# Whole-head and half-head cache loads in elements two to four of a two-layer decode kernel

## The chip, the cores and the metric

The kernel runs on one core of a Trainium2 chip. The metric is the device time of one execution in microseconds; the median over the runs is compared. The profile is of one execution. Its engines are PE (matmuls; PEld are its weight loads), DVE (VectorE), ACT (ScalarE), POOL (GpSimd) and SP (SyncE, which issues nearly all transfers).

## The reference

A decode step for four batch elements goes through two equal layers, each an attention block over a cache and a feed-forward block. The weights and the cache are the same in both layers.

```python
B, Sq, D = 4, 1, 512
Hq, Hkv, Sk, Dh = 32, 8, 4096, 128          # cache: [B, Hkv, Sk, Dh], bf16

def _A_ref(x, k_cache, v_cache, wq, wo):
    q = (x @ wq).reshape(B, Sq, Hq, Dh)      # moved to [B, Hq, Sq, Dh]
    k = jnp.repeat(k_cache, rep, axis=1)     # four query heads share a key head
    v = jnp.repeat(v_cache, rep, axis=1)
    scores = jnp.einsum("bhqd,bhkd->bhqk", q, k) * (Dh ** -0.5)
    p = _softmax(scores, axis=-1)
    o = jnp.einsum("bhqk,bhkd->bhqd", p, v)
    return o.reshape(B, Sq, Hq * Dh) @ wo

def _B_ref(x, w_gate, w_up, w_down):
    return (_gelu(x @ w_gate) * (x @ w_up)) @ w_down

x = x + _A_ref(_layernorm(x), k_cache, v_cache, wq, wo)
x = x + _B_ref(_layernorm(x), w_gate, w_up, w_down)
x = x + _A_ref(_layernorm(x), k_cache, v_cache, wq, wo)
x = x + _B_ref(_layernorm(x), w_gate, w_up, w_down)
```

The result does not depend on the order of the 4096 cache positions, so a kernel may put them on the partitions in any way that keys and values share.

## The kernel before

**Tiles.** One head of keys or values is 4096 x 128 in bf16, 1 MB. It is held as two tiles (t = 0 and 1, "half heads") of 512 KB, each 128 partitions x 16 positions x 128. In the usual layout tile t holds one contiguous half of the head, and each partition reads one run of 4 KB. In element one (b = 0), the heads of the first group (`whole`) are laid out over the partitions as whole heads: a partition reads 32 positions, one run of 8 KB, and both tiles come with one transfer (`load_head`).

**Groups and elements.** The eight key heads form two groups of four. The elements are worked through in order, and layer two of element b is woven into layer one of element b + 1 (`attend`), so that the keys of element b can stay on the chip for both. Layer one takes the groups in the order `first_groups[b]` (0, 1 for elements one and three; 1, 0 for two and four), layer two in the opposite order (`second_groups`). In each part of the code the first group of the order at hand is gx, the second gy.

**Keys.** There are 16 key tiles on the chip (8 MB): `KW` for group 0 and `KP` for group 1. `place` says which tile holds which half head. In `attend` layer two's scoring of the previous element goes over gx, then gy, with t = 0 and then t = 1 (line 592); each pass frees four tiles, and four half heads of the next element are loaded into them (line 518). DVE then turns each key tile in place in the order of loading (`turn`, line 537, 1.2 us a tile), and layer one scores them. Scoring a tile takes four matmuls of 32 columns. The columns of the PE array follow the head, so that tiles of different heads go side by side. Layer one scores gx one tile at a time and gy in runs of three tiles and one (`last_alone`).

Between elements one and two there are no free tiles to load into. `Early` therefore parks three key tiles of group 0 in PSUM and elsewhere, loads three half heads into their places, and brings the parked ones back, on ACT, DVE and POOL (lines 565 to 570), as scoring frees others.

**Values.** Eight value tiles form a ring (`VRing`, in pairs `VP`). `ring.seq` is the list of half heads in the order in which they are to be loaded; `pump` issues the next load when a slot is free, and every value step (`Values.step`, `Streamed.fill`) frees one and pumps. Layer two keeps the last three half heads of layer one (`kept`), parks two more in PSUM (`apart`), and reads the other eleven again: three of the second group (`own`) and the eight of the first group (`other`). The eight are consumed during the next dense block, one at each `prev.fill()`, between the steps of the feed-forward block (lines 309 and 791). In the last element, three transfers of 1 MB go into the space of the query weights instead (`pump_head`, line 724), and one head goes into two freed key tiles.

**Queue.** All loads are issued by SP in program order. A load waits on SP for the matmul that last read its tile, and for an earlier transfer that used the same semaphore.

**The end.** `attend_last` takes the values of the last element in the order kept, own, apart, other. After heads 4 and 5 of the last group come the output rows of four heads (`rows.heads`, line 405), then head 6 with its rows, then head 7, whose output goes through line 275. The last feed-forward block follows (`dense_last`).

Of the kernel before, what the change touches and what calls it, by code (L numbers as in the profile page):

```python
# [15 lines left out]
P = 128  # L16
# [14 lines left out]
WD_PARTS = (0, 6, 10, 12, 13, 14)  # L31
ROWS_A = 8
# [4 lines left out]
def kernel(  # L37
# [58 lines left out]
    KW = [wts.tile([P, NT, CH, Dh], BF16, name=f"kw{s}") for s in range(GH)]  # L96
    KP = [[wts.tile([P, 2, CH, Dh], BF16, name=f"kp{t}_{j}") for j in range(GH // 2)]
          for t in range(NT)]
# [22 lines left out]
    place = {(s, t): (KW[s], t) for s in range(GH) for t in range(NT)}  # L121
    place.update({(GH + s, t): (KP[t][s // 2], s % 2) for s in range(GH) for t in range(NT)})

    def k_tile(i, t):
        pair, n = place[i, t]
        return pair[:, n]
# [15 lines left out]
    def whole(b, kvh):  # L142
        return b == 0 and kvh < GH

    def load_head(cache, kvh, to):
        dq.dma_start(out=to.rearrange("p t c d -> p (t c d)"),
                     in_=cache[0, kvh].rearrange("(p r) d -> p (r d)", p=P))

    def cache_tile(cache, b, kvh, t):
        if whole(b, kvh):  # L150
            return cache[b, kvh].rearrange("(p t c) d -> t p c d", t=NT, p=P)[t]
        return cache[b, kvh].rearrange("(t p c) d -> t p c d", t=NT, p=P)[t]
# [287 lines left out]
    def flat(t, nb):  # L440
        return t[:, :, 0] if nb == 1 else t
# [52 lines left out]
    class Keys:  # L494


        def __init__(self, b, groups):
            self.b, self.groups, self.nl, self.nt = b, groups, 0, 0

        def tile(self, n):  # L500
            g, u = divmod(n, TG)
            if whole(self.b, self.groups[g] * GH):
                s, t = divmod(u, NT)
            else:
                t, s = divmod(u, GH)
            return self.groups[g] * GH + s, t

        def load_heads(self, count):
            for _ in range(count):
                kvh, t = self.tile(self.nl)  # L510
                self.nl += NT
                load_head(A_k_cache, kvh, KW[kvh])

        def load(self, count):
            for _ in range(count):
                kvh, t = self.tile(self.nl)
                self.nl += 1
                dq.dma_start(out=k_tile(kvh, t), in_=cache_tile(A_k_cache, self.b, kvh, t))

        def load_pairs(self, count):  # L520
            for _ in range(count):
                kvh, t = self.tile(self.nl)
                (to, n), (other, m) = place[kvh, t], place[kvh + 1, t]
                if to is not other or (n, m) != (0, 1):
                    self.load(2)
                    continue
                self.nl += 2
                pair = A_k_cache[self.b, kvh:kvh + 2].rearrange("h (t p c) d -> t p h c d",
                                                                t=NT, p=P)
                dq.dma_start(out=to[:], in_=pair[t])  # L530

        def turn(self, count=1):
            for _ in range(count):
                kvh, t = self.tile(self.nt)
                self.nt += 1
                words = k_tile(kvh, t).rearrange("p c d -> p (c d)").bitcast(FP32)
                nc.vector.transpose(out=words, in_=words)  # L537
# [40 lines left out]
    together = (tuple(range(GH)),)  # L578
    singly = tuple((s,) for s in range(GH))
    last_alone = (tuple(range(GH - 1)), (GH - 1,))  # L580

    def scores(sc, g, t, runs=together):
        for run in runs:
            scores_of(sc, g, [(s, t) for s in run])

    def scores_of(sc, g, run):
        for be in range(BE):
            for s, t in run:
                n = s * BE + be
                w0 = n * 2 * W + (W if t == 0 else 0)  # L590
                kt = k_tile(g * GH + s, t).rearrange("p c (b j e) -> p c b j e", b=NB, e=2)
# [90 lines left out]
    class VRing:  # L682
# [9 lines left out]
        def pump(self, spare=None):  # L692
            free = self.free if spare is None else spare
            while self.at < len(self.seq) and free:
                key = self.seq[self.at]
                if key[0] == 1 and whole(*key[1:3]):
                    own = [free.pop(0) for _ in range(NT)]
                    n = [i for i, v in enumerate(slots) if v is own[0]][0]
                    assert n % NT == 0 and own[1] is slots[n + 1]
                    load_head(A_v_cache, key[2], VP[n // NT])  # L700
                    for t in range(NT):
                        assert self.seq[self.at] == key[:3] + (t,)
                        self.at += 1
                        self.ready[key[:3] + (t,)] = (own[t], spare is None)
                    continue
                self.at += 1
                v = free.pop(0)
                dq.dma_start(out=v, in_=cache_tile(A_v_cache, *key[1:]))
                self.ready[key] = (v, spare is None)
# [11 lines left out]
        def pump_head(self, keys, pair):  # L721
            (layer, b, kvh, t), other = keys
            assert t == 0 and other == (layer, b, kvh, 1)
            dq.dma_start(out=pair,
                         in_=A_v_cache[b, kvh].rearrange("(t p c) d -> p t c d", t=NT, p=P))
# [233 lines left out]
    def attend_first():  # L959
# [11 lines left out]
        keys.load_heads(GH)  # L971
        load_wq(gy)
        keys.load(TG)
# [36 lines left out]
        scores(sc1, gy, 0, last_alone)  # L1010
        keys.turn(4)
        vals.step(3)
        scores(sc1, gy, 1, last_alone)
# [25 lines left out]
    class Early:  # L1039


        def __init__(self, b, groups):
# [3 lines left out]
            self.own = dict(place)  # L1046
            flat = [k_tile(c + s, last).rearrange("p c d -> p (c d)") for s in range(GH)]
            self.two = [Parked(flat[2], [(ps_h, "h", 2), (ps_x, "x", 2)]),
                        Parked(flat[3], [(pool, "ot", 2) for pool in ps_ot])]
            self.one = Parked(flat[1], [(ps_sc, "sc", 2), (pep, "pe", 4), (pep, "pl", 4, 1)])  # L1050
            place[a, 0], place[a + 1, 0] = self.own[c + 2, last], self.own[c + 3, last]
            place[a + 2, 0] = self.own[c + 1, last]
            self.keys = Keys(b, groups)
            self.keys.load_pairs(1)
            self.keys.load(1)
# [33 lines left out]
        def scores(self, sc, qy, norm):  # L1089
            gx, gy, own, keys = self.gx, self.gy, self.own, self.keys  # L1090
            a, c, last = gx * GH, gy * GH, NT - 1

            def home(i, t, freed):
                place[i, t] = own[freed]
                return k_tile(i, t).rearrange("p c d -> p (c d)")

            def load(i, t, freed):
                home(i, t, freed)
                assert keys.tile(keys.nl) == (i, t)
                keys.load(1)  # L1100

            def first(run):
                now = {(a + s, t): place[a + s, t] for s, t in run}
                place.update({k: own[k] for k in now})
                scores_of(sc, gx, run)
                place.update(now)
# [9 lines left out]
            to = home(c + 1, last, (a + 1, 0))  # L1116
            self.one.back(to, 1, nc.vector)
            self.one.back(to, 2, nc.gpsimd)
            self.two[0].back(home(c + 2, last, (a, 0)), 2)
# [453 lines left out]
```

## Time and profile before

| | |
|---|---|
| median of 3 runs | 268.06 us (267.89 to 269.08) |
| profiled execution | 268.99 us, of which span 267.2 us |
| mean granted TensorE clock | 0.866 |
| PE / DVE / ACT / POOL busy | 195.1 / 182.2 / 66.0 / 3.9 us |
| PE weight loads | 114.8 us |
| bytes read from HBM | 102.50 MB, 384 GB/s over the span |
| key loads of 512 KB / 1024 KB | 56 / 4 |
| value loads of 512 KB into the ring / 1024 KB into the ring / 1024 KB into weight space | 89 / 4 / 3 |

The rows of the page give each engine's busy share, the 40 slices show how it lies over the span, and the list of transfers gives sizes and the time from issue to landing. That time includes the time spent behind earlier transfers of the queue. The groups by line show how often an instruction ran, its mean duration, and what ended the idle time before it. Matmuls overlap, so that the sum of their durations is more than the time they take.

### The profile page before, as it was taken

Reading aid. Unit: us, or ns where it says so; the run is one execution under the profiler, and the core shown is the slowest. Engines: PE = TensorE matmul, PEld = TensorE weight load, DVE = VectorE, ACT = ScalarE, POOL = GpSimd, SP = SyncE. Lnnn points to the kernel's source line nnn. Section 1 sums busy time; section 2 is a strip of 40 time slices with the busy share of each in tenths; the row PEclk is TensorE's granted clock in tenths of the full one; section 3 lists DMA queues with packets and bytes.
Section 4 is the critical chain, followed back from the end, with each engine's and each line's share of the span. In section 5 each row is a group of like instructions: output and inputs, shape, how many; then the busy total and the mean of one; then the engine's idle time right before and its main releaser. Section 6 shows DMA issues by size and latency. Waiting matters only on the chain.

```text
span 267.2 us, 8596 instructions
## 1 busy us (share of the span) xinstructions
PE 195.1 (73%) x3767; PEld 114.8 (43%) x3775; DVE 182.2 (68%) x448; ACT 66.0 (25%) x136; POOL 3.9 (1%) x10
## 2 busy tenths in 40 slices
PE   1396246544689796989678968787788687888884
PEld 1333123322255453557436245464363354553563
DVE  3385955451335899884776998746769996568773
ACT  1001001100222422032323520304136103044642
POOL 2000000000001000000000000000000000000001
PEclk9998555655597959799999985899999979999999
DMA  7999999999994999999999999999999999999940
GB/s 244 432 416 421 423 429 417 408 385 406 413 412 177 394 416 417 420 417 400 390 414 416 416 419 421 416 415 375 403 418 418 421 415 418 420 405 405 413 160 3
DMA packets 30732, 103.05 MB, mean 386 GB/s; under 512 B 2788, under 2 KB 7144, under 8 KB 29672
## 3 DMA queue, kind: packets, MB, share of 16 engines
q1 hardware_dynamic: 30672, 102.51, 95.7%
q8 instruction: 29, 0.48, 0.6%
q14 instruction: 7, 0.06, 0.1%
q10 hardware_dynamic: 24, 0.01, 0.0%
HBM read 102.50 MB, written 0.00 MB: 384 GB/s over the span
## 4 chain that ended last, share of the span: by engine, by line
DMA 51%; PE 21%; DVE 16%; SPq 6%; ACT 3%; issue 3%; DVEq 0%
DMA v_t<-in_A_v_cache_dram 25%; DMA kp<-in_A_k_cache_dram 8%; DMA kw<-in_A_k_cache_dram 8%; PE sc L592 6%; DMA wu_sb<-in_B_w_up_dram 5%; DMA kw<-in_A_v_cache_dram 4%; SPq L161 4%; DVE kp L537 3%; PE ot L859 3%; DVE kw L537 3%; PE y L275 3%; PE so L791 2%; PE q L309 1%; DVE q L315 1%; DVE qb L360 1%
## 5 line engine op out<-in xcount | busy, mean ns | idle before, releaser
L592 PE MATMUL sc<-kw,qb 128*32 128x512 bf16 x244 | 39.6, 446 | 5.2 <-DVE kw L537 2.2
L592 PE MATMUL sc<-kp,qb 128*32 128x512 bf16 x268 | 40.1, 450 | 1.0 <-DVE kp L537 0.2
L592 PEld LDWEIGHTS <-qb 128*32 128x32 bf16 x512 | 23.1, 104 | 39.6 <-issue 21.4
L537 DVE STREAM_TRANSPOSE kw<-kw 128x1024 f32<-128x1024 f32 x32 | 38.0, 1215 | 0.7 <-DMA kw<-in_A_k_cache_dram 0.6
L537 DVE STREAM_TRANSPOSE kp<-kp 128x1024 f32<-128x1024 f32 x32 | 36.7, 1199 | 0.0
L859 PE MATMUL ot<-pe,v_t 128*128 128x32 bf16 (+1 forms) x896 | 30.0, 184 | 5.6 <-DMA v_t<-in_A_v_cache_dram 2.8
L859 PEld LDWEIGHTS <-v_t 128*128 128x128 bf16 x896 | 27.7, 100 | 13.7 <-issue 7.4
L614 ACT ACTIVATE pe<-sc,nl 128x512 bf16<-128x512 f32 x8 | 5.5, 687 | 85.9 <-DVE pe L611 67.6
L791 PE MATMUL so<-v_t,pe 128*32 128x256 bf16 x304 | 15.0, 319 | 13.6 <-DMA v_t<-in_A_v_cache_dram 11.6
L799 DVE STREAM_TRANSPOSE so<-so 128x512 f32<-128x512 f32 (+1 forms) x23 | 13.8, 599 | 11.1 <-PE so L791 11.1
L791 PEld LDWEIGHTS <-pe 128*32 128x32 bf16 x320 | 9.1, 105 | 19.4 <-issue 12.5
L602 DVE TENSOR_REDUCE pe<-sc 128x1 f32<-128x512 f32 x12 | 8.3, 691 | 9.2 <-PE sc L592 9.1
L405 PE MATMUL yr<-wo_sb,OT_bf 128*2 128x512 bf16 (+1 forms) x120 | 10.7, 425 | 4.9 <-DMA wo_sb<-in_A_wo_dram 4.9
L647 PE MATMUL x<-pe,ident_bf 128*32 128x128 bf16 x192 | 5.4, 233 | 11.8 <-DVE pe L622 11.8
L647 PEld LDWEIGHTS <-ident_bf 128*32 128x32 bf16 x256 | 5.3, 100 | 16.1 <-issue 14.1
L791 PE MATMUL so<-v_t,pl 128*32 128x256 bf16 x192 | 9.4, 275 | 3.3 <-DMA v_t<-in_A_v_cache_dram 3.3
L650 ACT CAST pe<-x 128x512 bf16<-128x512 f32 x12 | 7.0, 586 | 17.4 <-PE x L647 17.4
L275 PE MATMUL q<-xb,wq_sb 128*128 128x5 bf16 (+1 forms) x192 | 5.7, 173 | 6.5 <-DMA wq_sb<-in_A_wq_dram 6.5
L353 PE MATMUL qe<-q_bf,ident_bf 128*32 128x16 bf16 (+1 forms) x272 | 5.7, 176 | 5.6 <-DVE q_bf L335 2.9
L622 DVE STREAM_TRANSPOSE pe<-pe 128x512 bf16<-128x512 bf16 x12 | 8.4, 696 | 1.1 <-ACT pe L614 1.1
L275 PEld LDWEIGHTS <-wo_sb 128*128 128x128 bf16 x160 | 7.6, 101 | 3.3 <-DMA wo_sb<-in_A_wo_dram 2.6
L482 PEld LDWEIGHTS <-ident_bf 128*128 128x128 bf16 x63 | 5.2, 99 | 8.7 <-issue 4.3
(172 smaller groups left out, 255.2 us busy)
## 6 DMA issues: line engine op xcount, KB each, us to landing
v_t<-in_A_v_cache_dram SPq DMA_DIRECT2D x89, 512.0 KB, 8.5
kp<-in_A_k_cache_dram SPq DMA_DIRECT2D x32, 512.0 KB, 9.9
kw<-in_A_k_cache_dram SPq DMA_DIRECT2D x24, 512.0 KB, 9.6
wq_sb<-in_A_wq_dram SPq DMA_DIRECT2D x2, 2048.0 KB, 7.7
kw<-in_A_k_cache_dram SPq DMA_DIRECT2D x4, 1024.0 KB, 11.6
v_t<-in_A_v_cache_dram SPq DMA_DIRECT2D x4, 1024.0 KB, 14.2
wo_sb<-in_A_wo_dram SPq DMA_DIRECT2D x4, 1024.0 KB, 12.0
wq_sb<-in_A_v_cache_dram SPq DMA_DIRECT2D x3, 1024.0 KB, 11.8
```

Of the source, the lines that this page charges most:

```text
L161: dq.dma_start(out=wo_sb[:, i * n:(i + 1) * n], in_=wo_dram[:, i * n:(i + 1) * n])
L275: nc.tensor.matmul(dst, lhsT=lhsT, rhs=rhs, start=first, stop=last, skip_group_check=True)
L405: nc.tensor.matmul(self.rows[j:j + x.shape[1]], lhsT=x, rhs=wo_sb[:, i], start=self.n < QD, stop=True, skip_group_check=True)
L537: nc.vector.transpose(out=words, in_=words)
L592: nc.tensor.matmul(sc[s * QS:(s + 1) * QS], lhsT=qb[:, w0:w0 + 2 * W], rhs=kt[:, :, be // 2, :, be % 2], start=(t == 0 and be == 0), stop= ...
L602: nc.vector.tensor_reduce(out=m, in_=sc.rearrange("p c j -> p (c j)"), axis=AX.X, op=ALU.min if norm else ALU.max)
L622: nc.vector.transpose(out=flat, in_=flat)
L647: nc.tensor.matmul(x[a * QS:(a + 1) * QS, s], lhsT=ident_bf[:, s * QS:(s + 1) * QS], rhs=pT[:, a], start=True, stop=True, skip_group_check ...
L650: nc.scalar.copy(out=pe, in_=x.rearrange("p s t c h -> p (s t c h)"))
L791: nc.tensor.matmul(ps[d, :NW * QS], lhsT=x[:, w:w + NW].rearrange("p c h -> p (c h)"), rhs=v[:, i:i + NW, d], start=first and i == 0, stop ...
L799: nc.vector.transpose(out=flat, in_=flat)
L859: nc.tensor.matmul(self.ot[:, s % 2], lhsT=v[:, i, :], rhs=wide(pe[:, s, t * CH + i, :], self.ot.shape[-1]), start=(done == 0 and i == 0), ...
```

## The change

In elements two to four, the layout of whole heads is used for three of the four heads of the layer-one order's second group (all but `SPLIT_HEAD` = 2). Their keys come as whole heads of 1 MB in runs of 8 KB, their values in layer one likewise, and of the rereads in layer two the one head of which both halves are read again. All else stays in contiguous half heads. Element one is as before.

To have both halves of a head in one region, the 16 key tiles become eight regions of two (`KH`), and the regions 2 and 5 (`SPLIT`) may hold halves of different heads. `Keys` no longer computes the order of tiles but records it as it loads (`seq`). `load_free` runs after each pass of layer two's scoring of gy: it loads a half of head 2 when a tile in region 2 or 5 is free, and a whole head when both tiles of a region are. `Early` parks (3, 0), (3, 1) and (2, 1) instead of (1, 1), (2, 1) and (3, 1). Layer one's scoring goes by the recorded order. The ring's `pump` loads a whole head only when both slots of a pair are free, and halves go by preference into a slot whose partner is taken. The list of the ring changes too: the first half head of the next element goes ahead of the whole reread head; in the last element the whole reread head is the first `pump_head`, heads 4 and 5 follow, and head 6 goes through the ring.

The diff, cut to its core:

```diff
+SPLIT = (2, 5)
+SPLIT_HEAD = 2
...
-    KW = [wts.tile([P, NT, CH, Dh], BF16, name=f"kw{s}") for s in range(GH)]
-    KP = [[wts.tile([P, 2, CH, Dh], BF16, name=f"kp{t}_{j}") for j in range(GH // 2)]
-          for t in range(NT)]
+    KH = [wts.tile([P, NT, CH, Dh], BF16, name=f"kh{s}") for s in range(Hkv)]
...
-    def whole(b, kvh):
+    def as_head(b, kvh):
         return b == 0 and kvh < GH
 
-    def load_head(cache, kvh, to):
+    def adjacent_in(b, kvh):
+        if b == 0:
+            return as_head(b, kvh)
+        return kvh // GH == first_groups[b][1] and kvh % GH != SPLIT_HEAD
+
+    def load_head(cache, b, kvh, to):
         dq.dma_start(out=to.rearrange("p t c d -> p (t c d)"),
-                     in_=cache[0, kvh].rearrange("(p r) d -> p (r d)", p=P))
+                     in_=cache[b, kvh].rearrange("(p r) d -> p (r d)", p=P))
...
+        def load_free(self, g, t, homes):
+            self.free.update(homes)
+            for home in sorted(self.free):
+                if home[0] in SPLIT:
+                    self.free.remove(home)
+                    self.load_tile(g * GH + SPLIT_HEAD, self.half, home)
+                    self.half += 1
+            for region in range(Hkv):
+                pair = {(region, t) for t in range(NT)}
+                if pair <= self.free:
+                    self.free -= pair
+                    self.load_head(region, self.todo.pop(0))
...
+        def last_alone(self, lo, hi):
+            tiles = [u for run in self.singly(lo, hi) for u in run]
+            return [sorted(tiles[:-1], key=lambda u: u[1]), tiles[-1:]]
...
+        def pair(self):
+            for i in range(0, V_SLOTS, NT):
+                own = [self.find(v) for v in slots[i:i + NT]]
+                if None not in own:
+                    self.free = [v for v in self.free if v is not slots[i] and v is not slots[i + 1]]
+                    return i
+            return None
...
+                head = [key[:3] + (t,) for t in (range(NT) if key[0] == 1 else (1, 0))]
+                if adjacent_in(*key[1:3]) and self.seq[self.at:self.at + NT] == head and (
+                        key[0] == 1 or key[1] > 0):
+                    i = self.pair()
+                    if i is None:
+                        return
+                    load_head(A_v_cache, key[1], key[2], VP[i // NT])
...
-            self.two = [Parked(flat[2], [(ps_h, "h", 2), (ps_x, "x", 2)]),
-                        Parked(flat[3], [(pool, "ot", 2) for pool in ps_ot])]
-            self.one = Parked(flat[1], [(ps_sc, "sc", 2), (pep, "pe", 4), (pep, "pl", 4, 1)])
+            self.two = [Parked(flat(3, 0), [(ps_h, "h", 2), (ps_x, "x", 2)]),
+                        Parked(flat(3, last), [(pool, "ot", 2) for pool in ps_ot])]
+            self.one = Parked(flat(2, last), [(ps_sc, "sc", 2), (pep, "pe", 4), (pep, "pl", 4, 1)])
...
-        for t in range(NT):
-            scores(sc2[1], gy, t)
-            keys.load(GH)
+        score_and_load(sc2[1], gy, keys.load_free)
         ring.extend(1, b, one(b)[ahead_of[b]:])
         ring.extend(2, b - 1, other2)
-        ring.extend(2, b, own1)
+        ring.extend(2, b, own1[:1])
+        if b < B - 1:
+            ring.extend(1, b + 1, one(b + 1)[:1])
+            ring.extend(2, b, own1[1:])
+        else:
+            ring.extend(2, b, other1[2 * NT:3 * NT])
...
-        scores(sc1, gy, 0, last_alone)
+        for run in keys.last_alone(TG, TG + GH):
+            scores_of(sc1, gy, run)
         turn(4)
         vals1.step(3)
-        scores(sc1, gy, 1, last_alone)
+        for run in keys.last_alone(TG + GH, 2 * TG):
+            scores_of(sc1, gy, run)
...
-                ring.pump_head(late[:NT], pairs_of[0])
+                ring.pump_head(sorted((2, b) + u for u in two(b)[1][1:]), pairs_of[0])
...
-                ring.pump_head(late[NT:2 * NT], pairs_of[1])
-                ring.pump_head(late[2 * NT:3 * NT], pairs_of[2])
+                ring.pump_head(late[:NT], pairs_of[1])
+                ring.pump_head(late[NT:2 * NT], pairs_of[2])
...
-                ring.extend(1, b + 1, one(b + 1)[:ahead_of[b + 1]])
+                ring.extend(1, b + 1, one(b + 1)[1:ahead_of[b + 1]])
```

183 lines of the change are left out of this document (88 added, 95 removed).

## The prediction

> **What bounds the kernel now.** I read the page first: the rows of the DMA engines in the 40 slices and the queue's share.
>
> ```profile
> DMA  7999999999994999999999999999999999999940
> GB/s 244 432 416 421 423 429 417 408 385 406 413 412 177 394 416 417 420 417 400 390 414 416 416 419 421 416 415 375 403 418 418 421 415 418 420 405 405 413 160 3
> ...
> q1 hardware_dynamic: 30672, 102.51, 95.7%
> ```
>
> The sync engine's one queue moves 102.5 MB and is busy for 95.7% of the span. It stands still only in the first 2 us, in the hole of slice 13 (80.8 to 84.8 us) and after 258.3 us. So what moves the end is the time per byte, a new hole, or the work behind the last landing. The second view is the busy time by stretch (start:end, length, five engines, granted clock, DMA share, GB/s). I chose stretches in which one shape fills the queue, and then the three weakest later ones.
>
> ```profile
> 9.00:13.00 4.00, 1.64 (x67) 1.55 (x65) 2.14 (x6) 0.00 (x0) 0.00 (x0) 1.00 1.01 426
> 35.00:42.00 7.00, 3.75 (x52) 2.25 (x55) 3.46 (x6) 0.00 (x0) 0.00 (x0) 0.50 1.01 428
> 20.00:25.00 5.00, 3.15 (x29) 1.18 (x26) 3.31 (x7) 0.37 (x1) 0.00 (x0) 1.00 1.02 420
> 136.00:142.00 6.00, 4.69 (x89) 2.42 (x81) 3.73 (x10) 1.49 (x4) 0.00 (x0) 1.00 1.03 421
> 120.00:134.00 14.00, 11.61 (x292) 7.50 (x280) 8.46 (x32) 4.13 (x8) 0.00 (x0) 1.00 1.02 396
> 183.00:189.00 6.00, 3.89 (x136) 2.30 (x131) 4.23 (x16) 1.70 (x4) 0.00 (x0) 1.00 1.00 370
> 238.00:244.00 6.00, 4.51 (x136) 2.18 (x131) 4.61 (x17) 3.98 (x7) 0.00 (x0) 1.00 1.02 397
> ```
>
> Rows one and two are element one's whole heads in runs of 8 KB: 426 and 428 GB/s. Rows three and four are runs of 4 KB: 420 and 421. The last three are the dense blocks of elements two to four, where value slots come free one by one: 396, 370, 397. The key loads of 134 to 162 us (line 518) show how deep the queue is, and the chain of waits shows a dense block's loop: a slot freed at 180.81, its load landing, the matmul that waited.
>
> ```profile
> DMA to landing us min/median/max: 6.5/10.3/10.5
> ```
>
> ```profile
> 180.81 5.34 DMA v_t<-in_A_v_cache_dram
> 186.20 0.40 PE so L791 x8
> ```
>
> At 1.23 us between issues (152.33, 153.56, 154.78 in SP's timeline), 10.3 us is eight transfers in flight; 5.34 us is four. Last, PE's timeline near the end, and two scoring rows of the middle.
>
> ```profile
> 253.83 1.06 PE L791 MATMUL so<-wq_sb,pl 128*32 128x256 bf16 x32 [0.36 <-ACT pl L650]
> 254.71 1.04 PE L405 MATMUL yr<-wo_sb,OT_bf 128*4 128x512 bf16 x16
> 255.84 0.62 PE L791 MATMUL so<-wq_sb,pl 128*32 128x256 bf16 x16
> 256.29 0.60 PE L405 MATMUL yr<-wo_sb,OT_bf 128*4 128x512 bf16 x8
> 257.04 0.57 PE L859 MATMUL ot<-pl,kw 128*128 128x32 bf16 x16 [0.15 <-DMA kw<-in_A_v_cache_dram]
> 257.46 0.55 PE L275 MATMUL y<-OT_bf,wo_sb 128*128 128x32 bf16 x16
> 257.86 0.83 PE L859 MATMUL ot<-pl,kw 128*128 128x32 bf16 x16
> ```
>
> ```profile
> 150.72 1.02 PE L592 MATMUL sc<-kw,qb 128*32 128x512 bf16 x4 [0.23 <-DVE kw L537]
> 165.45 2.11 PE L592 MATMUL sc<-kp,qb 128*32 128x512 bf16 x16
> ```
>
> The first block shows heads 4 and 5 (253.83), two heads' output rows, head 6 as it lands (255.84; its landing is 255.8), then head 7 in two tiles. The second shows one tile alone: four matmuls in 1.02 us; and a group of sixteen in 2.11 us, where three heads go side by side and the fourth follows.
>
> **Runs of 8 KB (a gain).** Per element, three key heads, three value heads and one reread head, 21 heads or 22.02 MB in all, change from 4 KB to 8 KB runs. At 420.5 GB/s they take 52.37 us, at 427 GB/s 51.57 us: 0.80 us less, on the path, since the queue sets the end. The nearest pairs of rows bound it: 426 against 423 (161 to 167 us) gives 0.4 us, 428 against 419 (209 to 217 us) gives 1.1 us. I take the middle, from stretches of one shape. The 20 issues that fall away cost nothing: SP has 0.33 us of work per 1.23 us. [...]
>
> **Key loads moved behind the second scoring pass (nothing).** Layer two's scoring of group gy freed four tiles per pass and loaded them at once. Now a head waits for both of its halves: after the first pass 1.0, 1.5 and 0.5 MB go out in elements two, three and four, the rest after the second, which takes 1 us (32 matmuls in 2.00 us at 139.42). Cover: transfers in flight, at least 2.5 us of them at 88.10 (five loads issued since 83.10) and 8 to 10 us at 141 and 194. Without it each element would lose 1 us. In element two a parked tile, head 3's first half, must now be back for the first pass; ScalarE's second copy ends near 87.0 and that pass starts at 87.00: 0 to 0.2 us, hidden by the same 2.5 us.
>
> **Value heads that wait for a pair (nothing).** In elements three and four the first whole value head leaves at the third value step instead of the first, 160.34 to 163.63 us. What was issued then lands 9 to 10 us later, so at least 5 us stay queued without it. The reread head leaves at the seventh refill of a dense block instead of the fifth: some 2.4 us later for half of it, with four transfers queued.
>
> **Layer one's scoring in landing order (hidden in part).** The first three of four gy tiles now hold both halves of one head. Those share 32 columns, so eight matmuls follow one another instead of four: 8 x 0.255 against 4 x 0.255 us, +1.0 us per group, two groups per element. Cover: PE's waits for values before the element's end (in element three 0.62, 0.17 and 0.49 us, 1.3 in all). So 0.7 us is left, beside the next item and not on top of it.
>
> **The last value head lands whole (hidden by the queue).** Its first tile was usable one half earlier (177.45 against 178.87 us). Now both come at the second's landing, so each dense block starts 1.2 us later, less the gain collected so far: 1.0, 0.8 and 0.4 us. Cover: 5.34 us to landing at 180.81 is 4.1 us of queued work in front; 2.9 us or more stays. The matmul at 186.20 waits for a landing, not for the block. In element four PE waits for the block itself (0.25 us at 241.00), so 0.4 us goes on to 253.83; head 5 is late there anyway.
>
> **The end (a loss).** In element four the reread head takes the first of the three 1 MB transfers; heads 4 and 5 move one place back, and head 6 goes ahead in two ring slots. The transfer that landed at 255.8 us now carries head 5, not head 6. Behind head 6 PE had 1.20 us to head 7 (255.84 to 257.04). Behind head 5 come its own 0.45, sixteen row matmuls 1.0, head 6 0.45 and eight row matmuls 0.55: 2.45 us. Head 7 has landed by then, which saves the 0.3 us that its last piece kept PE waiting. Net 0.95 us; bounds 0 (if the order still hides) and 1.25.
>
> **Sum.** -0.80 + 0.95 + 0.05 = +0.2 us. The profiled execution took 268.99 us (span 267.2, 1.79 around it), 0.93 over the median; it becomes 269.2, and the median of 268.06 becomes **268.3 us**. Its own range is 267.0 to 269.3: the gain's 1.1 with no loss at the end, and the gain's 0.4 with 1.25 at the end and 0.4 more at the dense blocks. All of it is no change, since a measurement of this kernel can tell about 0.5% (1.3 us).
>
> **Rival one, slower: the dense blocks run the queue dry.** Its place is the first refills of each dense block (125.34, 180.81, 235.79). It decides once the shift passes 2.1 us: 5.34 us to landing, less the 3.2 us that a load into the empty queue took (issued 83.10, landed 86.31). Shifts from the scoring groups (2.0) and the whole head (1.2) would pass it if they add up: 1.1 us lost per block, 3.3 in all, and 271.6 us; half of that, 270.0, is the likelier case of it. For it: these blocks are already the weakest rows. Against: PE waits for landings there. [...]
>
> **Rival two, faster: the weak stretches fill up.** Against 420 GB/s the three rows lose 0.80, 0.71 and 0.33 us, 1.8 in all. Fewer and longer transfers under the same eight in flight hold more bytes, and next element's first value half now goes ahead of the reread head. If that fills them: -0.80 - 1.8 + 0.95 = -1.65, 266.4 us. Against: slots, not the count in flight, limit there.
>
> **Rival three: the end hides.** With 0.95 gone the gain of 0.8 stands alone: 267.3 us, still no change.
>
> **Numbers.** The forecast has 0.33, rival three 0.12, rival one 0.34, rival two 0.21. Range 266.1 to 270.9: it takes in both ends of the forecast, rival two and most of rival one. Faster 0.21, same 0.45, slower 0.34.
>
> **What would show it.** Right: stretches of whole heads at 426 to 428 GB/s; about 20 fewer issues; the last landing near 257.5 with 2.4 us of PE from head 5 to head 7; scoring groups of 3 us. Wrong: a DMA digit below 9 in a dense block or rates under 360 there (rival one), 410 or more there (rival two), head 7 waiting for its landing (rival three).

## The result, and the profile after

The changed kernel took 278.4 us (median of six runs, 276.2 to 282.4); the kernel before, run beside it, 268.4 us. The ratio is 1.033, 95% interval 1.027 to 1.040; it leaves out one disturbed run of the six, and so lies below the ratio of the medians. By it the change costs about 9 us. The forecast was 268.3 us with a range up to 270.9: wrong, and outside the range. Rival one, the dense blocks that run dry, had the direction and the place; its price (270.0 to 271.6 us) was far too small. Of the signs that the prediction had named, rates under 360 GB/s in a dense block (rival one's) came: 326 and 340.

The profiled execution took 276.22 us (span 274.3, so 7.1 more than before). The rows of the DMA engines in the 40 slices, and the queue's share:

```profile
DMA  6999999999978999999999999999999999999900
GB/s 256 432 416 420 424 429 415 401 386 414 409 313 300 422 417 418 401 329 409 409 401 417 430 413 415 410 394 341 392 417 423 421 416 422 401 329 388 361 10 3
...
q1 hardware_dynamic: 27664, 102.51, 93.8%
```

Outside the known hole (slices 12 and 13) there are new dips: 329 in slice 18, 341 in slice 28, 329, 388 and 361 in slices 36 to 38. The first four lie at the dense blocks of elements two, three and four, the last holds the end of the loading. The digits of busy share still read 9 there: these slices show a queue that runs low in their rate, and the digit did not fall. Five of the stretches of the prediction, then three longer ones that hold the dense blocks (start:end, length, busy time of five engines, granted clock, DMA share, GB/s):

```profile
9.00:13.00 4.00, 1.67 (x68) 1.59 (x66) 2.10 (x6) 0.00 (x0) 0.00 (x0) 1.00 1.02 430
35.00:42.00 7.00, 3.75 (x60) 2.40 (x63) 3.19 (x5) 0.00 (x0) 0.00 (x0) 0.65 1.01 428
120.00:134.00 14.00, 11.08 (x269) 7.18 (x261) 7.67 (x29) 3.77 (x6) 0.00 (x0) 1.00 0.99 367
183.00:189.00 6.00, 4.84 (x146) 2.88 (x137) 4.34 (x15) 2.99 (x5) 0.00 (x0) 1.00 0.97 326
238.00:244.00 6.00, 4.54 (x146) 2.85 (x142) 4.46 (x17) 3.19 (x5) 0.00 (x0) 1.00 0.94 340
...
112.00:144.00 32.00, 25.80 (x574) 15.75 (x571) 20.17 (x68) 8.12 (x18) 0.00 (x0) 1.00 1.01 387
176.00:202.00 26.00, 21.66 (x534) 14.13 (x523) 17.03 (x56) 7.11 (x15) 0.00 (x0) 0.99 1.00 381
234.00:252.00 18.00, 14.34 (x359) 8.71 (x357) 12.14 (x41) 7.93 (x17) 0.00 (x0) 1.00 0.97 369
```

Element one's stretches are unchanged. The dense blocks ran at 396, 370 and 397 GB/s before and run at 367, 326 and 340. In the three longer stretches the kernel before had 407, 403 and 407 GB/s. Against the 420 GB/s that the steady stretches of before showed, the shortfall (length times the missing share) was 1.0, 1.1 and 0.6 us and is 2.5, 2.4 and 2.2: 4.5 us more in the profiled execution. Some 0.7 us of that is made up elsewhere: the last landing comes 3.8 us later (262.11 against 258.28 us), and so does that of the last 1 MB transfer, which now carries head 5 (259.62 against 255.80). The other 3.2 of the 7.1 us lie behind that landing, below.

Two waits show where the blocks' shift begins. VectorE copies the first value head to its parking place, and it scales the output of the last value head. The copy in element three and the scaling in element four, before and then after, and the scaling in element three after:

```profile
169.86 0.69 DVE L554 TENSOR_SCALAR park<-v_t 128x512 int32<-128x512 int32 x1 [0.50 <-DMA v_t<-in_A_v_cache_dram]
234.53 0.17 DVE L680 TENSOR_TENSOR OL_bf<-ot,rden 128x16 bf16<-128x16 f32 x1 [1.23 <-PE ot L859]
...
171.26 0.70 DVE L565 TENSOR_SCALAR park<-v_t 128x512 int32<-128x512 int32 x1 [1.68 <-DMA v_t<-in_A_v_cache_dram]
...
237.55 0.17 DVE L686 TENSOR_TENSOR OL_bf<-ot,rden 128x16 bf16<-128x16 f32 x1 [2.46 <-PE ot L887]
...
180.92 0.17 DVE L686 TENSOR_TENSOR OL_bf<-ot,rden 128x16 bf16<-128x16 f32 x1 [1.11 <-PE ot L887]
```

The waits of 0.50 and 1.23 us became about 1.2 us longer, the time of one half head (1.23 us between issues in the steady queue): the first half lies inside a transfer that has not landed. The copy waits 1.68 us in elements three and four alike (before 0.50 and 0.43). The scaling does not: before it waited 1.23 us in each element, after 1.74, 1.11 and 2.46. Both stand ahead of the dense block, the copy even ahead of the softmax that the block's values need.

### The profile page after: what moved, and what is told of

Its sections match the earlier page's. It is cut to its first block, busy times and chain, and to the rows that moved or that the text cites. A ratio compares the mean times of both kernels' runs of the same rounds, so it can differ in the third digit from the quotient of the medians.

```text
span 274.3 us, 8557 instructions
## 1 busy us (share of the span) xinstructions
PE 198.1 (72%) x3775; PEld 116.7 (43%) x3775; DVE 182.4 (66%) x448; ACT 66.0 (24%) x136; POOL 3.9 (1%) x10
## 4 chain that ended last, share of the span: by engine, by line
DMA 45%; PE 23%; DVE 20%; SPq 6%; ACT 3%; issue 2%; DVEq 0%
DMA v_t<-in_A_v_cache_dram 27%; DVE kh L539 11%; DMA kh<-in_A_k_cache_dram 8%; PE sc L598 7%; PE ot L887 5%; DMA wu_sb<-in_B_w_up_dram 5%; DMA wq_sb<-in_A_v_cache_dram 5%; SPq L167 4%; PE so L819 2%; PE y L281 2%; PE yr L411 1%; PE q L315 1%; ACT pe L656 1%; DVE pe L608 1%; DVE q L321 1%
## 5 line engine op out<-in xcount | busy, mean ns | idle before, releaser
L539 DVE STREAM_TRANSPOSE kh<-kh 128x1024 f32<-128x1024 f32 x64 | 74.2, 1209 | 0.6 <-DMA kh<-in_A_k_cache_dram 0.6
L598 PE MATMUL sc<-kh,qb 128*32 128x512 bf16 x512 | 67.8, 427 | 6.7 <-DVE kh L539 2.9
L598 PEld LDWEIGHTS <-qb 128*32 128x32 bf16 x512 | 24.0, 101 | 40.7 <-issue 21.6
L887 PE MATMUL ot<-pe,v_t 128*128 128x32 bf16 (+1 forms) x896 | 29.1, 183 | 4.9 <-DMA v_t<-in_A_v_cache_dram 2.6
L411 PE MATMUL yr<-wo_sb,OT_bf 128*2 128x512 bf16 (+1 forms) x120 | 12.6, 496 | 5.0 <-DMA wo_sb<-in_A_wo_dram 5.0
L819 PE MATMUL so<-v_t,pl 128*32 128x256 bf16 x208 | 10.3, 285 | 2.6 <-DMA v_t<-in_A_v_cache_dram 2.6
L565 DVE TENSOR_SCALAR park<-v_t 128x512 int32<-128x512 int32 x12 | 7.8, 677 | 3.4 <-DMA v_t<-in_A_v_cache_dram 3.4
L819 PEld LDWEIGHTS <-pl 128*32 128x32 bf16 x240 | 5.8, 100 | 8.5 <-issue 5.8
```

Source lines behind the costliest of these rows:

```text
L411: nc.tensor.matmul(self.rows[j:j + x.shape[1]], lhsT=x, rhs=wo_sb[:, i], start=self.n < QD, stop=True, skip_group_check=True)
L598: nc.tensor.matmul(sc[s * QS:(s + 1) * QS], lhsT=qb[:, w0:w0 + 2 * W], rhs=kt[:, :, be // 2, :, be % 2], start=(t == 0 and be == 0), stop= ...
L819: nc.tensor.matmul(ps[d, :NW * QS], lhsT=x[:, w:w + NW].rearrange("p c h -> p (c h)"), rhs=v[:, i:i + NW, d], start=first and i == 0, stop ...
L887: nc.tensor.matmul(self.ot[:, s % 2], lhsT=v[:, i, :], rhs=wide(pe[:, s, t * CH + i, :], self.ot.shape[-1]), start=(done == 0 and i == 0), ...
```

## The experiments

The theory: whole value heads leave late and land late, and a dense block that starts later is paid for in full; the end of element four adds its part. Its rivals in the experiments (other than the prediction's own): the layout makes reading slower (called rival one in the first expectations), or the keys' late loads and longer scoring are the cause (rival two).

Costs are given as (ratio - 1) times 268.4 us, from the ratio to the kernel before that was run beside it; the intervals of the ratios are 0.3 to 1% wide to each side.

**One. Parts of the change undone.** Four kernels made from the changed one.

The end of element four as before (reread head in halves, heads 4, 5 and 6 in the late transfers):

```diff
-            ring.extend(2, b, other1[2 * NT:3 * NT])
+            ring.extend(2, b, own1[1:])
...
-                ring.pump_head(sorted((2, b) + u for u in two(b)[1][1:]), pairs_of[0])
+                ring.pump_head(late[:NT], pairs_of[0])
```

> The changed kernel with the order of before at the end of element four alone: the reread head goes back into two ring slots as halves, and the three late 1 MB transfers carry heads 4, 5 and 6 again. Theory (whole value heads leave and land late; the end is one part of it): the tail from the last but one landing shrinks from 6.1 us to about 3.1, and the three late transfers leave earlier; 2 to 3.5 us come back, 273 to 274.5 us in a profile that gave 276.2 before this edit. Rival one (runs of 8 KB, or halves at a stride of 8 KB, are themselves slow to read): about 1 us at the end, 275. Rival two (the keys' late loads and the shared columns of the scoring are the cause): below 1 us, 275.5 to 276.

Measured: 275.2 us, ratio 1.0244 (1.0203 to 1.0285). The end is worth some 2.3 us of the 8.9, uncertain by about 2 us; 6.5 us remain. The 273 to 274.5 us of the theory were counted from the profiled 276.2, the fastest of the change's runs; its 2 to 3.5 us came back, but rival one's 275 fits the time as well.

All values of elements two to four in halves as well, keys whole:

```diff
+    def whole_now(key):
+        return key[1] == 0
...
-                        key[0] == 1 or key[1] > 0):
+                        key[0] == 1 or key[1] > 0) and whole_now(key):
```

> The changed kernel with every value head of elements two to four in two half loads (runs of 4 KB at a stride of 8 KB), in the order of before, the end included. Keys stay whole heads. Theory (value heads that wait for a pair of slots and land whole): nearly all of the loss goes, 268.5 to 270.5 us. Rival one (halves at a stride of 8 KB are slow to read): little comes back, 274 to 277. Rival two (keys): only the end's part comes back, 273 to 275.

Measured: 270.4 us, ratio 1.0054 (1.0018 to 1.0090). Most of the loss is gone, as the theory had it.

Keys in halves, values whole:

```diff
-        score_and_load(sc2[1], gy, keys.load_free)
+        score_and_load(sc2[1], gy, keys.load_group)
```

> The changed kernel with the keys of the second group in half loads and in the loading order of before, so that the scoring runs as before too; values stay whole heads. Theory (values): 0 to 2 us come back, 274.5 to 276.5. Rival one (layout): no change, 276 to 277. Rival two (keys' late loads, scoring of 3.5 us in place of 2): most comes back, 270 to 272.

Measured: 279.0 us, ratio 1.0371 (1.0323 to 1.0419). Nothing comes back, and the theory's 0 to 2 us is missed too: rival two, the keys, falls.

Keys and values in halves:

> The changed kernel with keys and values of elements two to four all as half loads in the orders of before: only the layout of the halves is left of the change (runs of 4 KB at a stride of 8 KB, where before they lay end to end). Theory (values' waiting): as the kernel before, 268 to 269.5 us. Rival one (layout): still slow, 273 to 277. Rival two (keys): as the kernel before, 268 to 269.5.

Measured: 270.4 us, ratio 1.0070 (1.0045 to 1.0096). Theory and rival two both missed, and rival one got less than it asked: 1.9 us stay although no whole head is left in these elements. The next groups take that up; it also means that the kernels built on halves in the new layout carry a second effect.

**Two. One kind of whole head at a time, on the kernel with whole keys and halved values; and the end alone.**

```diff
-        return key[1] == 0
+        return key[1] == 0 or key[0] == 1 and key[2] % GH == GH - 1      # the last head
+        return key[1] == 0 or key[0] == 1 and key[2] % GH in (0, 1)      # the first two
+        return key[1] == 0 or key[0] == 2 and key[1] < B - 1             # the reread head
```

> Keys whole, all values in halves but one: the last value head of elements two to four (layer one, the head after which the element's output is finished) loads whole, when two slots are free. The same kernel with that head in halves too took 270.4 us; with the first two heads and the reread head whole as well it took 275.2. Theory (what delays the start of a dense block is paid in full, since the first refill of the block starts later and the queue has no cover): 1.2 us in each of three blocks, 273 to 274.5 us. Rival (the cover of 2.9 us that the prediction read from the first refill's time to landing): 270 to 271.

Measured: 274.2 us, ratio 1.0212 (1.0187 to 1.0237), 3.8 us above 270.4, as if each block paid for its later start in full; the third group tests that.

> Keys whole, all values in halves but the first two heads of the second group in elements two to four, which load whole, when two slots are free; the kernel with these in halves too took 270.4 us. Theory (a head that waits for its pair leaves late, the copy of its first half into a parking tile waits for its landing on VectorE, and the softmax behind it with it: 0.8 to 1.2 us in elements three and four): 271.5 to 273.5 us. Rival (the prediction: 5 us stay queued, nothing is lost): 270 to 271.

Measured: 274.8 us, ratio 1.0233 (1.0192 to 1.0274). More than the theory had.

> Keys whole, all values in halves but the reread head of elements two and three, which loads whole when two slots are free, behind the next element's first half, as in the change; element four and its end as before. The kernel with that head in halves too took 270.4 us. Theory (the refill in a dense block waits for its second slot, some 2.4 us for half of it, in two blocks, at a place where the queue already runs below its rate): 271.5 to 273 us. Rival (the prediction: four transfers are queued, nothing is lost): 270 to 271.

Measured: 270.8 us, runs from 269.5 to 274.6, ratio 1.0129 (1.0038 to 1.0220). By its medians nothing, by its ratio 2 us: undecided.

> Keys whole, all values in halves, the ring's order as before, but the end of element four as in the change: the reread head whole in the first late 1 MB transfer, heads 4 and 5 one place later, head 6 in two ring slots. The kernel with the end of before took 270.4 us. The prediction's step: 0.95 us, 271.4. Theory (head 5 is late, and heads 5, 6 and 7 with their output rows stand behind the last landings: 3 us): 272.5 to 274. Rival (the end hides): 270.4.

Measured: 271.5 us, ratio 1.0110 (1.0072 to 1.0148): 1.1 us above 270.4 by the medians. That is the prediction's 0.95, and my theory's 272.5 to 274 us are missed; inside the change the same end cost 2.3 by the ratios.

**Three. A dense block's cover, measured by itself.** Nothing of the change: in the kernel before, matmuls without a reader stand ahead of each of the three blocks (10 in one kernel, 20 in the other).

```diff
         assert vals1.left() == 0
+        busy(10, spare, start=False)
         rows.onto(proj)
```

> The kernel before with ten matmuls whose results nobody reads (128x256, about 0.12 us each) put behind the last value matmul of elements two to four, so that each of the three dense blocks starts about 1.1 us later; nothing else is changed. Theory (a dense block has no cover: its first matmuls free the slots that the queue waits for, and a shift of its start is paid in full): 3 times 1.1 us less what falls beside other waits, 270.5 to 272. Rival (a cover of 2.9 us): as before, 268 to 269.

> The same with twenty such matmuls, about 2.3 us per dense block. Theory (no cover): 273.5 to 275.5 us. Rival (a cover of 2.9 us): 268 to 269; with a cover of 1 us: twice the cost of the kernel with ten less 3 us, near 272.

VectorE's first instruction of element three's block, with the delay of 10 and then of 20 (before: at 180.47, after a wait of 0.74):

```profile
182.04 0.17 DVE L425 TENSOR_TENSOR xb<-XX,y 128x4 bf16<-128x4 f32 x1 [1.64 <-PE y L275]
```

```profile
183.76 0.17 DVE L425 TENSOR_TENSOR xb<-XX,y 128x4 bf16<-128x4 f32 x1 [2.73 <-PE y L275]
```

Each block starts 0.9 and 2.0 us later by its own wait. Measured: 271.1 us, ratio 1.0094 (1.0067 to 1.0121), and 275.4 us, ratio 1.0262 (1.0223 to 1.0300); so 2.5 and 7.0 us, against 2.7 and 6.0 for three shifts paid in full (uncertain by 0.7 and 1.0). Over the kernel none of it is covered that these runs can tell. The stretch 183 to 189 us of the kernel with 20 shows where it goes:

```profile
183.00:189.00 6.00, 4.82 (x160) 3.36 (x157) 4.24 (x16) 3.19 (x5) 0.00 (x0) 1.00 0.84 283
```

Before it was 370 GB/s. In SP's timeline of this block, in the kernel before, eight refills leave between 180.81 and 189.2 us, as the block's steps free the slots, and the first key load, which waits for the scoring behind the block, at 190.52. That is one load in 1.2 us, the pace of the steady queue itself (1.23 us between issues), so a queue that has become shallow is not filled up within the block.

Issue and landing of the single transfers show what becomes of the shift. Before, four transfers are in flight whenever a refill leaves, and the refills land 1.2 to 1.6 us apart. With the delay of 10 three are in flight at each of the first three refills, with 20 two, and landings come up to 2.1 and 2.2 us apart. Compared with before, the first refill lands 0.67 and 1.48 us later, about as much as the last load ahead of the block (0.70 and 1.35); the eighth lands 1.63 and 3.52 us later. So the first refill is covered and the later ones are not: the queue slows down before it is empty, and by the end of the block it has lost the whole shift.

**Four. The same question from the other side.** Can an earlier start be gained? The last value half goes in two transfers of 256 KB.

```diff
+                if key[0] == 1 and key[1] > 0 and key[2:] == one(key[1])[-1]:
+                    self.pump_halves(key, v)
```

> The kernel before with the last value half of layer one in elements two to four in two transfers of 256 KB, so that half of its sixteen matmuls are done before its end has landed. If a shift of a dense block's start is paid in full, an earlier start is gained: 0.3 us in each of three blocks, 267.5 us (267.2 to 268). Rival (a block's start counts only when it is late): 268.4, or 268.6 with the price of the shorter runs.

Measured: 269.1 us, ratio 1.0041 (1.0008 to 1.0074): no gain, and a little above the rival's time too. The premise was wrong: the sixteen matmuls of that half still ran in one piece, at 177.85 us right behind PE's output rows, and the wait of the scaling behind them stayed at 1.25 us. In the kernel before, the last half is there by the time PE comes to it.

**Five. What the layout costs.** The kernel before with other addresses alone.

```diff
-        if whole(b, kvh):
+        if whole(b, kvh) or strided(b, kvh):
             return cache[b, kvh].rearrange("(p t c) d -> t p c d", t=NT, p=P)[t]
```

> The kernel before with other addresses alone: the halves of the second group's keys and values in elements two to four are read in runs of 4 KB at a stride of 8 KB, where before they lay end to end; order, sizes, slots and homes as before. It asks where the 1.9 us go by which the changed kernel in halves (270.4) stands above the kernel before. Theory (they go to the tiles' other homes and the slots' other order; a stride costs nothing, since the steady stretches of both ran at 416 to 420 GB/s): 268 to 268.8 us. Rival one (the stride itself costs): 270 to 270.8.

Measured: 270.6 us, ratio 1.0090 (1.0058 to 1.0123). The layout's rival is right about these halves: a stride of 8 KB alone costs some 2.4 us. Two of its stretches (before: 407 and 418 GB/s):

```profile
90.00:95.00 5.00, 3.64 (x125) 3.38 (x121) 4.86 (x13) 1.49 (x4) 0.00 (x0) 0.89 1.01 368
...
144.00:176.00 32.00, 25.30 (x407) 13.73 (x403) 26.99 (x49) 8.29 (x15) 0.00 (x0) 0.84 1.02 415
```

In the long steady stretch, which holds such halves among others, the stride costs under 1%. The first one lies just behind the hole, where key halves arrive: 0.5 us is lost there. All four kernels with strided keys have it (331 to 368 GB/s), and none of the others (392 or more). With the keys alone at a stride:

```diff
-        if whole(b, kvh) or strided(b, kvh):
+        if whole(b, kvh) or strided(b, kvh) and cache is A_k_cache:
```

> The kernel before with the keys alone of the second group in elements two to four read in halves at a stride of 8 KB; values keep their addresses, so that scores and values belong to different tokens and the output is another one. With keys and values at a stride it took 270.6 us. If the keys make it (their loads at 91 to 94 us ran at 300 GB/s there): 270 to 270.8. If the values make it (they are loaded and reread in the dense blocks): 268 to 269.

Measured: 269.0 us, ratio 1.0023 (0.9992 to 1.0054). The keys' part, 0.6 us (its interval takes in zero), is about what that stretch loses; the larger part comes with the values, as their forecast had it, and no one stretch shows it. Why is open. None of this is in the changed kernel, which reads no such half in these elements.

**Six. Waiting for two slots, landing in one piece, or the layout?** Addresses, key loads and end of before; the whole value heads as 1 MB transfers in runs of 4 KB.

```diff
+    def in_one(b, kvh):
+        return b > 0 and kvh // GH == first_groups[b][1] and kvh % GH in WHOLE
...
+                        dq.dma_start(out=VP[i // NT][:], in_=A_v_cache[key[1], key[2]].rearrange(
+                            "(t p c) d -> p t c d", t=NT, p=P))
```

> Addresses and key loads of before, the end of before; the value heads that the change loads whole (three per element, and the reread head of elements two and three) go as one transfer of 1 MB when two slots are free, but in runs of 4 KB, as the addresses of before give them. The kernel before took 268.3 us, the change with the end of before 275.2. Theory (waiting for two slots and landing in one piece is what costs, whatever the layout): 274.5 to 276.5 us. Rival (the layout of 8 KB runs costs): 268.5 to 270.5.

Measured: 275.7 us, ratio 1.0243 (1.0177 to 1.0309): as with the change less its end (1.0244). So runs of 8 KB, whole keys, the loads moved behind the second pass and the scoring in landing order together came to nothing that these runs can tell (about 2 us), and the value transfers of 1 MB are the 6.5 us.

The last head alone (`WHOLE = (3,)`), then the first two (`WHOLE = (0, 1)`):

> The same with the last value head alone as one transfer of 1 MB (three transfers in the run), all else in halves. Theory: the dense block starts one half's time later, 1.2 us, and a delay of 0.9 us put there by itself cost 2.7 us in three blocks: 3 to 4 us, 271.5 to 272.5. Rival (the 3.8 us that this head cost among strided halves were the strides' doing): 268.5 to 270.

> The same with the first two value heads alone as transfers of 1 MB. Theory (they leave late and land in one piece; the parking copy waits on VectorE, ahead of the softmax): 3 to 5 us, 271.5 to 273.5. Rival (only the strides beside them cost): 268.5 to 270.

Measured: 273.1 us, ratio 1.0160 (1.0100 to 1.0220), and 272.0 us, ratio 1.0107 (1.0033 to 1.0181): 4.3 and 2.9 us by the ratios, 7.2 together, about the 6.5 of all. The last head came out above both its forecasts, the first two heads within the theory's. The two waits separate cleanly. Scaling of the last head in element three with the last head whole (before: 179.55, wait 1.23):

```profile
181.33 0.17 DVE L690 TENSOR_TENSOR OL_bf<-ot,rden 128x16 bf16<-128x16 f32 x1 [2.56 <-PE ot L897]
```

Parking copies of elements three and four with the first two whole (before: waits of 0.50 and 0.43):

```profile
170.03 0.69 DVE L569 TENSOR_SCALAR park<-v_t 128x512 int32<-128x512 int32 x1 [1.77 <-DMA v_t<-in_A_v_cache_dram]
...
226.49 0.69 DVE L569 TENSOR_SCALAR park<-v_t 128x512 int32<-128x512 int32 x1 [1.69 <-DMA v_t<-in_A_v_cache_dram]
```

The wait for two slots kept, the landing in one piece taken away:

```diff
-                        dq.dma_start(out=VP[i // NT][:], in_=A_v_cache[key[1], key[2]].rearrange(
-                            "(t p c) d -> p t c d", t=NT, p=P))
+                        for t in (range(NT) if key[0] == 1 else (1, 0)):
+                            dq.dma_start(out=slots[i + t], in_=cache_tile(A_v_cache, *key[1:3], t))
```

> As the kernel with all those heads in 1 MB transfers, but when two slots are free the head goes as two halves, one behind the other: the wait for two slots is kept, the landing in one piece is gone. If the late leaving alone costs: as with whole transfers, 274 to 276 us. If the landing in one piece is most of it (the last head's first half can be used 1.2 us before its second, and so can the parked half): 269.5 to 271.5. By theory the first heads cost through both and the last head through landing alone: 271 to 273.

Measured: 269.9 us beside 269.3 of the kernel before, ratio 1.0021 (0.9986 to 1.0056). This is the decisive run. Its heads still wait for two slots (the first of element three leaves at 162.82 us, before at 160.34), in the same order, and that costs nothing that can be told, at most 1.5 us; both waits are back at their old lengths:

```profile
169.50 0.69 DVE L569 TENSOR_SCALAR park<-v_t 128x512 int32<-128x512 int32 x1 [0.42 <-DMA v_t<-in_A_v_cache_dram]
...
179.12 0.17 DVE L690 TENSOR_TENSOR OL_bf<-ot,rden 128x16 bf16<-128x16 f32 x1 [1.27 <-PE ot L897]
```

My own theory had given the late leaving a share (271 to 273 us); these runs show none. Last, a whole head that is neither parked nor last (`WHOLE = (1,)`):

> Addresses, key loads and end of before; the second value head alone as one transfer of 1 MB in elements two to four (three transfers). It is neither parked nor last. Theory (a whole head costs where its first half would be used before the second has landed; the first two together cost 2.7 us, all of it by the parking copy): 268 to 269.5 us beside 268.3 to 269.3 of the kernel before. Rival (a transfer of 1 MB costs wherever it stands): 270 to 271.

Measured: 269.4 us, ratio 1.0027 (1.0000 to 1.0055). A whole head costs little where its first half is not wanted early; by difference some 2.2 of the 2.9 us of the first two heads are the parked head's, uncertain by about 2 us, since the parked head was not run alone.

No run beat the kernel before, and none points to one that would: with the gain of 8 KB runs too small to tell and halves in that layout slower, its 268.4 us stand.

## Why the prediction was wrong

**The runs of 8 KB (predicted -0.80).** The rates are right: 430 and 428 GB/s in element one, and 426 from 150 to 160 us, where whole heads arrive now, against 419 before. The gain didn't reach the end: whole keys against halved keys (270.4 and 270.4 us) and the comparison in group six show none, within about 2 us.

**Key loads moved (nothing).** Held.

**Value heads that wait for a pair (nothing).** Held for the waiting, by the decisive run, to within 1.5 us. What the step did not ask is what the head does when it lands: the copy of its first half to the parking place waits on VectorE for the whole transfer, 1.2 us longer in elements three and four, ahead of the softmax. That term is missing from the sum, by difference about 2.2 us. The prediction had both halves come at the second's landing for the last head alone; the copy's waits of 1.68 to 1.77 us, before 0.43 and 0.50, show the same for the first.

**Scoring in landing order (+1.0 per group, 0.7 left).** The size was right for the first group of an element. In the chain of waits after:

```profile
161.10 3.53 PE sc L598 x15
```

The first groups of elements two and four took 3.60 and 3.53 us, before 2.64 and 2.66: +0.9, about as forecast. The second groups, which were forecast to lose as much, took 1.95 to 2.04 us, before 1.55 to 2.40: on the whole no longer. And with keys in halves, and the scoring as before, nothing came back (279.0 us): it lies beside other work.

**The last value head lands whole (hidden by a cover of 2.9 us).** This is the step that failed. The shift of 1.2 us per block was right: with the last head alone whole, the scaling waited 2.43, 2.56 and 2.50 us in the three elements, before 1.23. The cover was not there. It was read from the first refill's 5.34 us to landing, as if the queue kept its full rate until that time was used up. The delay kernels show that this holds for the first refill alone. Behind it a queue that is three or two deep in place of four landed its loads further apart (up to 2.1 and 2.2 us, before 1.2 to 1.6), and the eighth refill was late by the whole shift (1.63 and 3.52 us). The row that the prediction itself showed, 370 GB/s from 183 to 189 us, was a sign of it: with four in flight the queue fell below the 420 GB/s of its steady stretches in part of the block even without a shift. Three shifts of 1.2 us are 3.6; the last head alone cost 3.8 by its medians. In the change itself the scaling waited longer in two of three elements only, so there its share may be smaller. The point of decision of the prediction's rival one (a shift over 2.1 us) fell with the same step: the delay kernels lose from the first 0.9 us on.

**The end (+0.95, bounds 0 to 1.25).** The mechanism was right, and alone it had the predicted size: 1.1 us, with 2.46 us of PE from head 5 to head 7. In the change the same way took 4.39 us. PE's timeline:

```profile
259.66 1.05 PE L819 MATMUL so<-wq_sb,pl 128*32 128x256 bf16 x16 [1.73 <-DMA wq_sb<-in_A_v_cache_dram]
260.47 1.95 PE L411 MATMUL yr<-wo_sb,OT_bf 128*4 128x512 bf16 x16
262.17 1.09 PE L819 MATMUL so<-v_t,pl 128*32 128x256 bf16 x16
263.03 1.09 PE L411 MATMUL yr<-wo_sb,OT_bf 128*4 128x512 bf16 x8
264.05 0.61 PE L887 MATMUL ot<-pl,kh 128*128 128x32 bf16 x16
```

The sixteen output rows took 1.95 us, before 1.04. The stretches around it give the reason (granted clock third from the end):

```profile
256.00:260.00 4.00, 1.45 (x38) 1.06 (x30) 1.90 (x7) 2.49 (x4) 0.00 (x0) 0.79 0.94 371
260.00:264.00 4.00, 4.00 (x56) 1.91 (x47) 1.78 (x5) 0.00 (x0) 0.00 (x0) 0.50 0.07 27
```

PE was busy for 1.45 of 4 us while it waited for late transfers, and was then granted half its clock (0.50) just where its work is the path. In the kernel with the end alone PE was busy for 2.08 of 4 us and the clock stayed at 1.00; in the one with keys in halves and this end it fell to 0.61. Behind head 5 the end so cost 3.2 us in this execution and 1.3 in the kernel with the end alone, each above the 1.20 us of before. That the late transfers let the clock fall is what these three traces suggest; no experiment sets it apart. What they show is the rate: at a granted 0.50 the sixteen rows took 1.9 times as long, behind waits of 0.83 and 1.73 us.

**Together.** By the ratios the last head makes 4.3, the first heads 2.9 and the end 2.3 us: 9.5 against 8.9 measured. Each of the three is uncertain by about 2 us, so this is agreement and not proof that the parts add. Among strided halves they did not: the last and the first heads alone cost 3.8 and 4.4 us by their medians, all whole values together 4.8 (275.2 against 270.4). The prediction had +0.2, of which 0.05 stands in no step of it.

## What to carry to other kernels

Do not read cover from the time to landing of a block's first transfer. Look at how many transfers are in flight and whether the rate holds: here four in flight held it in part of the block only (370 GB/s from 183 to 189 us), with three and two the landings came up to 2.1 and 2.2 us apart, and a delay ahead of the block was paid in full, in each round (0.9 and 2.0 us at each of three blocks cost 2.5 and 7.0). The larger transfer was not usable in parts here (the copy of a first half waited 1.68 to 1.77 us in place of 0.43 and 0.50), so before merging two loads look for who uses the first half before the second has landed; waiting to issue them was cheap (at most 1.5 us), landing as one was not (6.5 us with the wait for two slots). Work that ends the program behind a wait for data should be priced at the full and at the half clock, since here it ran at a granted 1.00 with the end alone and at 0.50 in the change.

## What the runs showed of the hardware

Three things had not been expected. A queue that moved a half head in 1.2 us with eight in flight slowed before it was empty: with two to four in flight as a refill left, landings came up to 2.2 us apart. Halves of 4 KB runs at a stride of 8 KB ran at nearly the same rate in a long steady stretch that holds them among others (415 against 418 GB/s) but at 331 to 368 against 407 for five microseconds behind the hole, and cost 2.4 us over the kernel, most of it not located. The busy share of the DMA engines shows little of a queue that runs low: in the stretch from 183 to 189 us it was 0.97 at 326 GB/s after the change and 0.84 at 283 with the delay of 20, against 1.00 at 370 before. The rate is the row to read.
